# Attention, Fourier mixing and a feed-forward on one core: tying the squares of the scale passes to the feed-forward

## The chip, the core and the metric

One core of a Trainium2 chip. The metric is the device time of one execution in microseconds (us), and a kernel is judged by the median of several executions. The core's engines are named as in the profile: PE is TensorE (PEld its weight loads), DVE is VectorE, ACT is ScalarE, POOL is GpSimd, SP is SyncE, which here only issues DMAs. Each engine works through a queue of its own in order, and a name with a q (ACTq, SPq) is the queue's own work.

## What is computed

For 8 batches with 8 heads, 576 positions and head width 64, cut to what matters:

```python
scores = scale * q @ k.T + bias            # causal, window of 128 positions
x = softmax(scores) @ v                    # heads joined: [8, 576, 512]
u = x + real(fft2(x))                      # over positions and channels
un = (u - mean(u)) / sqrt(var(u) + 1e-6)
out = u + relu(un @ w1) @ w2               # w1 [512, 2048], w2 [2048, 512]
```

## The kernel before, in words

The kernel keeps products exact enough by splitting each operand into two f16 halves, so most products are three matmuls. For that every tensor has to be scaled to a good range first. For batches 2 to 7 a **scale pass** (`batch_scales`, line 254) reads q, k and v of the batch once ahead of time, in 15 pieces of up to 512 columns (5 of q, 5 of k, 5 of v):

- `fetch` (line 266) takes one of the slots in `mslots` (three of them once the second weight is ready, otherwise two), and SP loads a piece into it. For batches 3 to 7 a one-element POOL copy at line 272 first writes into the slot from `last[-1]`, the output of the last emitted attention weighting (line 491, DVE). The load writes the same slot, so it can't start before that copy.
- `part` (line 275) frees the slot in the plan and issues one ACT Square over the piece in place (line 278), with the sum of each row put in one column of the tile `mx`. A sum read-out (ACTIVATION_READ_ACCUMULATOR) goes with it.
- `top` and `scale` (lines 280 and 285) reduce `mx` on DVE (line 282), sum it over partitions with one matmul, and make the batch's scales; the batch's conversions to f16 (line 378) need them.

The **feed-forward** (`ffn`, line 735) goes over row sets of 256 (for odd batches also one of 128). Per row set it first makes blocks of 512 columns in one of two PSUM banks `fp` (line 752, 24 matmuls each). Each block is emptied by an ACT rectification (line 757) into one of eight slots of `hbuf`, and by a DVE subtraction that reads the bank and the rectified half and writes the second half (it runs through the helper at line 169). Only then can PE use the bank again. After the blocks of a row set, the second product (line 767) runs, in which there are no rectifications. Its sums leave the same two banks through a DVE instruction into `X` or `ut`. The bursts of line 752 and of line 767 alternate, each half as long as a row set.

**What sets the order.** All parts of the program are put into one heap with due times (`put`, line 165) and emitted in order of these. The unit of the due times is a planner's step: one pair of heads takes 6 of them and one batch 24. For batch b > 2 the k-th square is due at T + 24(b - 2) - 0.163 + 1.152 k (from `SB`, `SE`, `begin_of`, with T = `T1`), and the load of that piece 1.9 x 1.152 earlier. At that time the feed-forward of batch b - 3 is being emitted; its steps begin at T + 24(b - 2) + 0.432 and come every 24/64 (even batches) or 24/80 (odd ones), and the m-th rectification of its first burst falls on step 2m + 1, counted from m = 0. The order of emission is not the order in the queues: the framework places each engine's instructions at build time from a simulated timeline, in which an instruction goes into its queue when what it needs is there (`schedule_with_timeline_sim=True`, line 932). So a square can stand in ACT's queue ahead of rectifications that were emitted before it.

Around them on ACT are the exponentials of the attention (line 169), the first halves of their f16 pairs (line 428), conversions (line 378) and evictions of the Fourier products (lines 606 and 644 to 648). On SP are the loads and the DMA transposes of attention weights (line 437) and of normalised rows (line 729). POOL has little else: the copies of line 272, memsets (lines 263 and 642) and a power of the normalisation (line 712).

Of the kernel before, what the change touches and what calls it, by code (L numbers as in the profile page):

```python
# [22 lines left out]
NF = 2  # L23
# [59 lines left out]
def attn_fft_ffn_kernel(  # L83
# [16 lines left out]
    V, A, G, T = nc.vector, nc.scalar, nc.gpsimd, nc.tensor  # L100
# [40 lines left out]
    def w1_ap(e, c, f):  # L141
        g, o = divmod(f, 2)
        return wf[0][:, g, e, o * 512 + c * 128:o * 512 + c * 128 + 128]

    def w2_ap(e, f):
        g, o = divmod(f, 2)
        return wf[1][:, g, e, o * 512:(o + 1) * 512]
# [4 lines left out]
    def total(m):  # L152
        sums = ps_d.tile([128, 512], F32, name="pd")[:, 0:m.shape[1]]
        T.matmul(sums, misc[:, 7:8].broadcast_to([128, 128]), m, start=True, stop=True)
        return sums

    def root_inv(dst, src):
        V.tensor_scalar(dst, src, 0.5, 2.0 ** -81, ALU.mult, ALU.max)
        V.tensor_scalar(dst.bitcast(I32), dst.bitcast(I32), 1, 0x3F800000, ALU.logical_shift_right, ALU.bitwise_and)
        V.reciprocal(dst, dst)  # L160
# [4 lines left out]
    def put(t, f, *a):  # L165
        heappush(queue, (t, next(order), f, a))

    def after(dt, f, *a, **kw):
        put(now[0] + dt, lambda: f(*a, **kw))  # L169
# [3 lines left out]

    ready = set()
    weighed, valued = [0] * B, [0] * 4 * B
    last = []

    def weights(wi, t0, dt, t1, dt1):
        w, top = ((w1, 2.0 ** 7), (w2, 2.0 ** 14))[wi]
# [70 lines left out]
    def x_scales(sc, gi, r):  # L250
        V.tensor_scalar_mul(sc[:, 5:6], r, 2.0 ** -53)
        V.reciprocal(gi[:, 1:2], sc[:, 5:6])
        V.tensor_scalar_mul(sc[:, 6:7], gi[:, 1:2], 2.0 ** -3)
        V.tensor_scalar_mul(sc[:, 7:8], gi[:, 1:2], 2.0 ** -11)
# [3 lines left out]
    def batch_scales(b, t0, dt):  # L258
        box = {}

        def begin():
            box["mx"] = small.tile([128, 3, 5], F32, name="mx", tag="mx")
            G.memset(box["mx"], 0.0)

        def fetch(x, fl, o, n):
            assert (0, 7) in ready
            slot = next(turns) % (3 if (1, 7) in ready and b > NF else 2)
            assert slot not in held
            held.add(slot)
            box[x] = slot, mslots[slot][:, 0:n]  # L270
            if b > NF:
                G.tensor_copy(box[x][1][0:1, 0:1], last[-1])  # L272
            nc.sync.dma_start(out=box[x][1], in_=fl[:, o:o + n])

        def part(x, i, c):
            slot, t = box.pop(x)
            held.discard(slot)
            A.activation(t, t, AF.Square, accum_out=box["mx"][:, i, c:c + 1])  # L278

        def top():  # L280
            m1 = small.tile([128, 3], F32, name="m1")
            V.tensor_reduce(m1, box["mx"], AX.X, ALU.max)
            box["sums"] = total(m1)

        def scale():
            r = small.tile([128, 3], F32, name="r")
            root_inv(r, box["sums"])
            sc = small.tile([128, 8], F32, name="sc", bufs=3)
            V.tensor_scalar_mul(sc[:, 0:1], r[:, 0:1], 2.0 ** -58)
            V.tensor_scalar_mul(sc[:, 1:3], r[:, 1:3], 2.0 ** -51)  # L290
            V.scalar_tensor_tensor(sc[:, 3:4], sc[:, 0:1], 8.0, sc[:, 1:2], ALU.mult, ALU.mult)
            gi = small.tile([128, 8], F32, name="gi")
            V.reciprocal(gi[:, 0:1], sc[:, 3:4])
            nsl = small.tile([128, 12], F32, name="nsl")
            V.tensor_scalar(nsl[:, 0:8], slope_sb[:, 0:8], gi[:, 0:1], None, ALU.mult)
            V.tensor_scalar(nsl[:, 8:12], slope_sb[:, 8:12], sc[:, 0:1], None, ALU.mult)
            rg = att.tile([128, 1152], BF16, name="rg", bufs=2)
            A.activation(rg, rel_sb, AF.Copy, scale=sc[:, 3:4])
            x_scales(sc, gi, r[:, 2:3])
            scs[b] = sc, nsl, rg  # L300

        put(t0 - 2.5 * dt, begin)
        x = 0
        for i, (src, n) in enumerate(((q, NQ * 4), (k, NK * 4), (v, 2560))):
            fl = src[b].rearrange(("j p s -> (j p s)", "h p c d -> (h p c d)")[i == 2])
            fl = fl.rearrange("(p x) -> p x", p=128)
            for c, o in enumerate(range(0, n, 512)):
                put(t0 + dt * (x - (FL if b > NF else min(FL, 1.95))), fetch, x, fl, o, min(512, n - o))
                put(t0 + dt * x, part, x, i, c)
                x += 1  # L310
        put(t0 + dt * x, top)
        put(t0 + dt * x + 0.6, scale)
# [424 lines left out]
    def ffn(b):  # L737
        X = Xs[b]
        parts = [(uTs[b][i], 256, [X[:, XS[2 * i]], X[:, XS[2 * i + 1]]], 4 * b + 2 * i) for i in range(2)]
        if b % 2 == 1:  # L740
            parts.append((uTs[b][2], 128, [uts[b // 2]], 4 * B + b // 2))
        for uT, n, tiles, slot in parts:
            per = 512 // n
            hh = []
            assert (b, id(uT)) in ready
            for f0 in range(0, 16, per):
                assert (0, (f0 + per - 1) // 2) in ready
                fp = ps_f.tile([128, 512], F32, name="fp")
                for i in range(per):
                    for c in range(4):  # L750
                        for p, (e, j) in enumerate(((0, 0), (0, 1), (1, 0))):
                            T.matmul(fp[:, i * n:(i + 1) * n], w1_ap(e, c, f0 + i), uT[:, j, c, 0:n],  # L752
                                     start=(c == 0 and p == 0), stop=(c == 3 and p == 2))
                    if i == per // 2 - 1:
                        yield
                ht = next(hslots)
                A.activation(ht[:, 0], fp, AF.Relu)  # L757
                after(0.2, V.scalar_tensor_tensor, ht[:, 1], fp, 0.0, ht[:, 0], ALU.max, ALU.subtract)
                for i in range(per):
                    hh.append(ht[:, :, i * n:(i + 1) * n])  # L760
                yield
            for i, t in enumerate(tiles):
                op = ps_f.tile([128, 512], F32, name="fp")
                for f in range(16):
                    assert (1, f // 2) in ready
                    for p, (a, e) in enumerate(((0, 0), (0, 1), (1, 0))):
                        T.matmul(op, hh[f][:, a, i * 128:(i + 1) * 128], w2_ap(e, f),  # L767
                                 start=(f == 0 and p == 0), stop=(f == 15 and p == 2))
                    if f % 2 == 1 and f < 15:
                        yield  # L770
                after(0.15, V.scalar_tensor_tensor, t, op, wone, t, ALU.mult, ALU.add)
                after(0.4, nc.sync.dma_start, out=ov[slot + i], in_=t)
                yield


    for p in range(4 * B):
        b, j = divmod(p, 4)
# [31 lines left out]
    for b in range(B):  # L809
        t = begin_of(4 * b)  # L810
        if b >= NF:
            batch_scales(b, *((t - SA, SD) if b == NF else (t - SB, SE)))
        fourier(b, transform_of(b))
        n = 80 if b % 2 else 64
        t = forward_of(b)
        put(t, step, ffn(b), t, (24 if b else forward_of(1) - t - E0) / n)
# [118 lines left out]
```

## Time and profile before

| what | value |
|---|---|
| median of 3 runs | 1081.24 us (1079.13 to 1081.65) |
| span of the profiled execution | 1083.9 us |
| PE busy in it | 1039.0 us (96%) |
| DVE, ACT, POOL busy | 703.2, 583.0, 48.0 us |
| squares of line 278 | 90 (75 of them of batches 3 to 7) |
| copies of line 272 | 75 |

The profiled execution's own time is known by its span alone, 1083.9 us from the first to the last instruction, which is 2.7 us (0.25%) above the median of the runs. A row of instructions reads: line, engine, operation, tile written <- tiles read, size, count; a bracket behind it gives how long its engine had been idle before it and what released it. In the table of stretches the columns are busy us and instruction count of each engine, then PEclk, the TensorE clock granted as a share of full speed (1.0 is 2.4 GHz, 0.5 is 1.2 GHz), and the DMA share.

### The profile page before, as it was taken

The page shows a single profiled execution, that of the slowest core. Times are in us where ns is not written, and L with a number is a line of the kernel's source. Part 1 is how long each engine was busy: PE and PEld are TensorE (multiplying, and loading weights), DVE is VectorE, ACT ScalarE, POOL GpSimd, SP SyncE. Part 2 cuts the span into 40 slices and gives each one's busy share as a digit, 9 for nine tenths or more (in the row PEclk, how much of TensorE's full clock was granted, in tenths as well). Part 3 has the DMA queues.
Part 4 walks back from the last instruction along what each step waited for, and adds up shares of the span by engine and source line. Part 5 has one row for each costly group of instructions (what it writes and reads, how often), then busy time and mean ns, then how long its engine had stood idle before and what let it go on. Part 6 is the DMA issues. An engine that isn't in the chain of part 4 may idle for free.

```text
span 1083.9 us, 23935 instructions
## 1 busy us (share of the span) xinstructions
PE 1039.0 (96%) x9208; PEld 726.4 (67%) x9208; DVE 703.2 (65%) x2073; ACT 583.0 (54%) x1388; POOL 48.0 (4%) x136
## 2 busy tenths in 40 slices
PE   8998889899899999999899999999999999999998
PEld 5876776675667667675657667584757676757655
DVE  4889789687674868687674858678784836252111
ACT  6886987558444567567554556556544522241000
POOL 0000001000000000001100000001000000000000
PEclk8998989999999999999999999999999999999999
DMA  9961466727542364527643364537522330030000
GB/s 365 346 218 56 123 147 158 151 54 187 136 101 75 97 147 123 147 51 152 170 109 74 96 146 119 143 54 134 110 60 34 53 69 11 10 60 11 20 10 21
DMA packets 191506, 117.81 MB, mean 109 GB/s; under 512 B 154400, under 2 KB 164128, under 8 KB 191392
## 3 DMA queue, kind: packets, MB, share of 16 engines
q1 hardware_dynamic: 190816, 114.84, 42.4%
q8 instruction: 72, 1.18, 0.5%
q10 hardware_dynamic: 576, 1.45, 0.3%
q14 instruction: 42, 0.34, 0.1%
HBM read 70.63 MB, written 9.44 MB: 74 GB/s over the span
## 4 chain that ended last, share of the span: by engine, by line
PE 61%; DVE 16%; DMA 9%; ACT 7%; issue 3%; SPq 2%; POOL 1%; ACTq 0%; DVEq 0%; POOLq 0%
PE fp L752 25%; PE fp L767 22%; PE sp L403 4%; DMA wall<-v_dram 4%; DVE P L415 2%; DMA wall<-q_dram 2%; ACT wall L278 2%; PE pd L602 2%; PE pv L468 2%; DVE P L169 1%; PE pd L636 1%; DVE hbuf L169 1%; DMA pt<-P 1%; ACT P L169 1%; PE sp L446 1%
## 5 line engine op out<-in xcount | busy, mean ns | idle before, releaser
L767 PE MATMUL fp<-wall,hbuf 128*128 128x512 f16 x1728 | 391.2, 379 | 0.0
L752 PEld LDWEIGHTS <-wall 128*128 128x128 f16 x3840 | 338.5, 99 | 70.4 <-issue 25.2
L752 PE MATMUL fp<-uT,wall 128*128 128x256 f16 x3072 | 365.4, 275 | 20.2 <-DVE hbuf L169 11.9
L767 PEld LDWEIGHTS <-hbuf 128*128 128x128 f16 x1728 | 162.8, 98 | 184.9 <-issue 3.5
L757 ACT ACTIVATE hbuf<-fp 128x512 f16<-128x512 f32 x144 | 84.8, 589 | 202.0 <-PE fp L752 201.9
L169 ACT ACTIVATE P<-P,nb 128x256 f32<-128x256 f32 x320 | 141.9, 477 | 60.8 <-DVE nb L415 60.5
L169 DVE SCALAR_TENSOR_TENSOR hbuf<-fp,hbuf 128x512 f16<-128x512 f32 x144 | 98.8, 686 | 99.3 <-ACT hbuf L757 98.4
L169 DVE SCALAR_TENSOR_TENSOR P<-P 128x256 f16<-128x256 f32 x240 | 87.4, 391 | 40.4 <-ACT P L428 38.9
L415 DVE CUSTOM_DVE_ANT_0 P<-sp,rg,nsl 128x256 f32<-128x256 f32 x240 | 97.5, 449 | 13.7 <-PE sp L403 12.0
L278 ACT ACTIVATE wall<-wall 128x512 f32<-128x512 f32 (+2 forms) x90 | 54.4, 605 | 91.3 <-DMA wall<-k_dram 33.5
L403 PE MATMUL sp<-kk,qq 64*128 64x256 f16 (+5 forms) x880 | 95.0, 287 | 1.4 <-ACT pt L449 0.7
L428 ACT ACTIVATE P<-P 128x256 f16<-128x256 f32 x240 | 84.1, 382 | 2.4 <-DMA pt<-P 1.7
L473 PE MATMUL pv<-vhs,pt 128*128 128x65 f16 x432 | 56.0, 195 | 1.2 <-DMA pt<-P 1.1
L474 PE MATMUL pv<-vl,pt 128*128 128x64 f16 x432 | 55.9, 193 | 0.0
L169 DVE SCALAR_TENSOR_TENSOR X<-fp,misc,X 128x512 f32<-128x512 f32 x32 | 23.8, 744 | 48.4 <-PE fp L767 48.3
L475 PE MATMUL pv<-vhs,pt 128*128 128x65 f16 x432 | 55.1, 194 | 0.0
L403 PEld LDWEIGHTS <-qq 64*128 64x128 f16 (+1 forms) x720 | 32.4, 99 | 24.6 <-issue 18.8
L473 PEld LDWEIGHTS <-pt 128*128 128x128 f16 x432 | 41.0, 98 | 9.6 <-issue 1.3
L752 PE MATMUL fp<-wall,wall 128*128 128x128 f16 x768 | 46.2, 219 | 0.0
L474 PEld LDWEIGHTS <-pt 128*128 128x128 f16 x432 | 40.7, 99 | 6.1
L468 PEld LDWEIGHTS pv<-vr,pt 128*128 128x128 f32 x288 | 37.6, 199 | 6.1 <-PE pv L323 3.3
L272 POOL COPY wall<-X 1x1 f32<-1x1 f32 x75 | 26.2, 377 | 343.9 <-DVE X L491 265.0
(159 smaller groups left out, 1205.9 us busy)
## 6 DMA issues: line engine op xcount, KB each, us to landing
qr<-q_dram SPq DMA_DIRECT2D x32, 304.0 KB, 3.2
hbuf<-w_dram SPq DMA_DIRECT2D x16, 512.0 KB, 7.7
out_dram<-X SPq DMA_DIRECT2D x32, 256.0 KB, 2.2
wall<-v_dram SPq DMA_DIRECT2D x30, 256.0 KB, 3.5
vr<-v_dram SPq DMA_DIRECT2D x24, 320.0 KB, 4.1
kr<-k_dram SPq DMA_DIRECT2D x24, 289.0 KB, 3.8
wall<-q_dram SPq DMA_DIRECT2D x24, 256.0 KB, 3.0
wall<-k_dram SPq DMA_DIRECT2D x24, 256.0 KB, 3.1
```

The source lines that it names most:

```text
L169: put(now[0] + dt, lambda: f(*a, **kw))
L278: A.activation(t, t, AF.Square, accum_out=box["mx"][:, i, c:c + 1])
L403: T.matmul(sp[e][:m, col:col + n], qq[h, c0:c0 + m], keys(kk[h], ti), start=(x == 0), stop=(x == len(prods) - 1))
L415: V.tensor_tensor_reduce(pt[:m, 0:n], sp[e][:m, col:col + n], tab[:m, pc:pc + n], mul, 3.0e38, ALU.add, ALU.min, nb[:m, ti:ti + 1])
L428: A.activation(hi, P32, AF.Copy, scale=2.0 ** 14)
L468: T.matmul(pv[:, ti], pt[:, col:col + 128], ops[p][2][:, e, vc], start=first, stop=last)
L473: T.matmul(pv[:, ti], ph, vh[:, e, vc], start=first, stop=False)
L474: T.matmul(pv[:, ti, 0:D], ph, vl[:, e, vc], start=False, stop=False)
L475: T.matmul(pv[:, ti], pl, vh[:, e, vc], start=False, stop=last)
L752: T.matmul(fp[:, i * n:(i + 1) * n], w1_ap(e, c, f0 + i), uT[:, j, c, 0:n], start=(c == 0 and p == 0), stop=(c == 3 and p == 2))
L757: A.activation(ht[:, 0], fp, AF.Relu)
L767: T.matmul(op, hh[f][:, a, i * 128:(i + 1) * 128], w2_ap(e, f), start=(f == 0 and p == 0), stop=(f == 15 and p == 2))
```

## The change

Every square of batches 3 to 7 gets a one-element POOL copy in front of it. It reads one element of the last rectification that was emitted, and writes it to the element of `mx` into which the square then puts its first row's sum. So the square can't be placed before that rectification and the copy. The list `pace` collects the rectified tiles in order of emission.

```diff
-    last = []
+    last, pace = [], []
...
         def part(x, i, c):
             slot, t = box.pop(x)
             held.discard(slot)
+            if b > NF:
+                G.tensor_copy(box["mx"][0:1, i, c:c + 1], pace[-1])
             A.activation(t, t, AF.Square, accum_out=box["mx"][:, i, c:c + 1])
...
                 ht = next(hslots)
                 A.activation(ht[:, 0], fp, AF.Relu)
+                pace.append(ht[0:1, 0, 0:1])
                 after(0.2, V.scalar_tensor_tensor, ht[:, 1], fp, 0.0, ht[:, 0], ALU.max, ALU.subtract)
```

## Rows read from the trace of the kernel before

**Rows 1.** The page, part 1: busy us, share of the span, instructions of each engine

```profile
PE 1039.0 (96%) x9208; PEld 726.4 (67%) x9208; DVE 703.2 (65%) x2073; ACT 583.0 (54%) x1388; POOL 48.0 (4%) x136
```

**Rows 2.** Waits of PE, 195 to 735 us: us in total, times, longest us

```profile
PE fp L752 <- DVE hbuf L169: 11.9, 10, 2.7
PE fp L752 <- DVE ut L169: 3.5, 2, 2.5
PE pd L602 <- DVE zl L610: 3.5, 3, 2.1
PE fp L752 <- DVE X L169: 2.0, 2, 1.4
PE pv L473 <- DMA pt<-P: 1.1, 1, 1.1
PE pd L602 <- ACT fh L575: 0.8, 1, 0.8
```

**Rows 3.** Line 278, 145 to 735 us: ACT's idle us before it, times

```profile
  DMA wall<-k_dram: 33.5, 17
  DMA wall<-q_dram: 28.4, 13
  DMA wall<-v_dram: 26.3, 12
```

**Rows 4.** Timeline of ACT, 395.5 to 403.9 us: start us, us, instruction

```profile
397.30 0.63 ACT L278 ACTIVATE wall<-wall 128x512 f32<-128x512 f32 x1 [4.32 <-DMA wall<-q_dram]
...
400.31 0.57 ACT L757 ACTIVATE hbuf<-fp 128x512 f16<-128x512 f32 x1
403.20 0.60 ACT L757 ACTIVATE hbuf<-fp 128x512 f16<-128x512 f32 x1 [2.32 <-PE fp L752]
```

**Rows 5.** Timeline of SP's queue, 388 to 398 us

```profile
390.22 2.63 SPq L729 DMA_TRANSPOSE uT<-un  x2
```

**Rows 6.** ACT's idle time before line 278, 391.55 to 424 us, then 449 to 453 us

```profile
  DMA wall<-q_dram: 6.1, 2
  DMA wall<-k_dram: 3.3, 2
...
  DMA wall<-v_dram: 6.0, 2
```

**Rows 7.** Timeline of PE: four places between 275 and 650 us

```profile
275.19 2.79 PE L752 MATMUL fp<-uT,wall 128*128 128x256 f16 x24
...
280.86 2.41 PE L752 MATMUL fp<-uT,wall 128*128 128x256 f16 x12 [2.67 <-DVE hbuf L169]
...
511.82 0.38 PE L752 MATMUL fp<-uT,wall 128*128 128x256 f16 x2 [1.44 <-DVE X L169]
...
646.07 4.45 PE L752 MATMUL fp<-uT,wall 128*128 128x256 f16 x24 [2.48 <-DVE ut L169]
```

**Rows 8.** Busy time by stretch: 645.2 to 648.6 us

```profile
645.20:648.60 3.40, 2.53 (x14) 1.88 (x14) 2.04 (x5) 1.37 (x5) 0.00 (x0) 0.68 0.89 253
```

**Rows 9.** The page, part 5: the copies of line 272 (busy us, mean ns, POOL idle)

```profile
L272 POOL COPY wall<-X 1x1 f32<-1x1 f32 x75 | 26.2, 377 | 343.9 <-DVE X L491 265.0
```

**Rows 10.** The page, part 6: loads of k's pieces (count, KB, us to landing)

```profile
wall<-k_dram SPq DMA_DIRECT2D x24, 256.0 KB, 3.1
```

**Rows 11.** Timeline of POOL, 535 to 540 us

```profile
535.31 3.39 POOL L272 COPY wall<-X 1x1 f32<-1x1 f32 x2 [18.41 <-DVE X L491]
```

**Rows 12.** Timeline of DVE, 535.9 to 538.8 us

```profile
537.04 0.67 DVE L538 TENSOR_TENSOR fg<-X 128x512 f32<-128x512 f32 x1
```

**Rows 13.** Timeline of ACT: the end of batch 5's pass and a later rectification

```profile
452.51 0.19 ACT L278 ACTIVATION_READ_ACCUMULATOR wall<-wall 128x1 f32 x1
...
470.68 0.60 ACT L757 ACTIVATE hbuf<-fp 128x512 f16<-128x512 f32 x1 [0.96 <-PE fp L752]
```

**Rows 14.** Timeline of DVE: the reduction and the scales of batch 5

```profile
452.73 0.17 DVE L282 TENSOR_REDUCE m<-mx 128x3 f32<-128x15 f32 x1 [6.28 <-ACT wall L278]
...
481.03 0.15 DVE L159 TENSOR_SCALAR r<-r 128x3 int32<-128x3 int32 x1
```

## The prediction

> **What bounds the kernel.** The page first: PE is busy for 96% of the span, ACT for 54%, POOL for 4% [rows 1]. So only PE's gaps can be won or made longer. PE's waits come next, in the stretch where batches 3 to 7 are scaled [rows 2]: 22.8 us in all. Most end with the DVE instruction that frees a feed-forward bank (11.9, 3.5 and 2.0 us) or with a Fourier half that waits for ACT (3.5 us).
>
> Then the view of line 278, to see what ACT was doing: before the 75 squares of batches 3 to 7 ACT sat idle for 33.5 + 28.4 + 26.3 = 88.2 us, each time until a load had landed [rows 3]. The timelines join the two. At 397.30 a square of batch 5 starts after 4.32 us of waiting for q's piece. Its load was late because SP had been issuing two transposes for 2.63 us [rows 5]. Behind it in ACT's queue stand work of the attention and the rectification of 400.31 [rows 4]. The same picture stands ahead of 280.86 us, where PE's next block starts 2.67 us late [rows 7].
>
> These gaps have a second price. After the two longest, 2.67 and 2.48 us [rows 7], the granted clock fell: 0.68 over the mean of one 3.4 us stretch, so part of it at 1.2 GHz instead of 2.4 [rows 8]. There 24 matmuls took 4.45 us where they take 2.79 at full clock [rows 7]: 1.7 us more, about 3.3 us for the two places.
>
> **Which squares move.** I worked out from the due times which rectification each square is tied to, and looked where both stand in ACT's queue. Example, batch 5, third q piece (k = 2): due at T + 72 + 2.14. Rectifications of batch 2's first burst are due at T + 72 + 0.81, 1.56, 2.31. So it is tied to the second, which ran at 403.20, while the square ran at 397.30: it moves past two rectifications and 5.9 us [rows 4]. So done for all 75, 50 squares stand ahead of their rectification (6 in batch 3, 11 in each of the others), by one to six rectifications and mostly 5 to 20 us. The other 25 are tied to one that ran long before, since they fall into bursts of line 767, and the tie does nothing. Of the waiting, 59.0 us stand before the 50 (4.8, 12.4, 15.4, 11.2, 15.1 us by batch) and 29.4 us before the 25. Batch 5 shows the reading: 6.1 + 3.3 us before its squares 1 to 8 and 6.0 us before the last three are its 15.4 us [rows 6].
>
> **What that takes away.** Of PE's 22.8 us I leave out three waits: 1.44 us at 511.82, where no square had waited for 5 us before [rows 7], and the 1.1 and 0.8 us for transposed weights and a Fourier input [rows 2]. The remaining 19.5 us follow, in the timelines, on a wait of one of the 50 squares. With the clock that is 19.5 + 3.3 = 22.8 us, the most the change can give back. The exchange rate from ACT to PE is 19.5 / 59.0 = 0.33: two thirds of ACT's waiting is hidden behind PE's second bank. The 29.4 us before the other squares cost PE nothing that I can see, and stay.
>
> **What it adds.** 75 POOL copies. POOL has time (mean 377 ns, 26 us for 75 [rows 9]), so they cost nothing there. Their price is that a moved square now stands in ACT's queue until rectification, copy and hand-overs are done, and the next exponential or rectification stands behind it. No row of before shows ACT waiting for such a copy. The lower bound is nothing, when ACT has other work in between. The upper is a square right behind its rectification: 377 ns and about 0.1 us for two hand-overs (DVE starts 0.03 us after the read-out of the last square ends [rows 13, 14]). I take that upper value, 50 x 0.48 = 24 us of ACT, since ACT is often idle just before it, and 0.33 of it for PE: 8 us. If PE hid none of it, it would be 24 us; if all, 0. Below nothing it can't be, since the order's own gain is already counted.
>
> **What is late next.** A square frees its slot later, and the load three pieces on waits for it. Most such loads wait longer for the weighting anyway: POOL sat idle 265.0 us for line 491 before line 272 [rows 9]. Where two squares three apart hang on neighbouring rectifications (the ninth piece of batches 4 to 7, tied to the end of a burst) the load starts only then. With 3.1 us to landing [rows 10] and SP's issue of up to 2.6 us [rows 5], each may bring back 2 to 4 us of ACT: some 12 us, or 4 us for PE. SP's queue holds the transposes of line 437 behind a load that waits. That risk is in the kernel already, as the load waits for POOL now too, and I cost it at nothing. It would cost PE a wait for transposed weights, of which there are 1.1 us now [rows 2].
>
> **The end of the pass** is covered. In batch 5 the last three squares move from before 452.70 to behind the rectification of 470.68 [rows 13], so the reduction comes near 473 instead of 452.73. The first instruction that needs its result starts at 481.03 [rows 14], held up by the single bank of the Fourier products, so 8 us are left. Batches 4 and 6 have more. The eight slots of `hbuf` now have a third reader, whose copy runs long before the slot comes round: nothing.
>
> **Sum.** 22.8 - 8 - 4 = 10.8 us less. The profiled span would go from 1083.9 to 1073; its offset of 2.7 us to the median stays, so the median goes from 1081.24 to about 1071 us. As the queues are placed anew at build time, other instructions will shift too. I have no row to size that; it is the blur in the bounds. With nothing lost the time is 1058; with 24 us for the copies and 4 for loads it is 1086.
>
> **The rivals.** A measurement of this kernel can tell 0.3% (3.2 us) from no change.
>
> *The waits come back* (no change). The slot chain makes every load as late as its square, or the squares behind a rectification wait for something else, so ACT idles as long. For it: three slots, and loads that already land late through SP [rows 5]. Against: the 5 to 20 us by which squares move are more than their waits of 1 to 5 us. If half of the 22.8 us goes and copies and loads cost 8 + 4 us, the change is about nil: 1081 us.
>
> *The copy holds ACT* (slower). POOL's queue is in order, too. A copy of line 272 waits in it up to 18.41 us for a weighting, and two copies there took 3.39 us [rows 11] while DVE ran a series of instructions with two SBUF inputs [rows 12]. If a rectification's copy stands behind these, the square and everything after it in ACT's queue stand still. The point of decision is a mean hold of 22.8 / (50 x 0.33) = 1.4 us per moved square, against the 0.48 I took. At 2 us it costs 33 us and gives 1081.2 + 10 = 1091 us. Against it: the builder puts POOL's copies in the order in which their inputs arrive in its timeline, and the mean copy was 0.377 us.
>
> A rule speaks for this rival. The Trainium skill (SBUF — State Buffer, "SBUF: two separate sides") says that DVE and GpSimd share a port pair as an exclusive lock, so that a GpSimd operation fully blocks behind a DVE instruction with two SBUF inputs. By that rule a copy takes as long as the DVE run beside it, and rows 11 and 12 agree. By it the sum would be slower only if most copies met such runs, as few of the 75 did, which their mean says.
>
> *The tie does nothing*, so the order stays. The copy's input and output are tracked like any other, so I give this almost nothing; it would be the no-change case.
>
> **How the numbers follow.** My forecast, faster, has 0.64: the waits are seen in rows and the moved squares are far from their loads. No change has 0.15, slower by more than 0.3% has 0.21. The likeliest time is 1071.0 us. The range reaches from 1060 (copies almost free) to 1087, which holds the no-change case and about half of the slower one. The forecast's own range is 1060 to 1078.
>
> **What would show it.** Right: ACT's idle time for loads before line 278 falls from 88 to some 40 us, the squares stand behind rectifications in the timeline, waits for POOL before line 278 stay near 25 us in all, PE's waits for `hbuf`, `X`, `ut` and `zl` fall from 20.9 to some 10 us, and the clock holds at 280 and 646 us. Wrong: long idle times of ACT released by line 278's copy, or as much waiting for loads as now; or PE waits elsewhere, for transposed weights or scales, because the new order is worse in a place that these rows do not show.

## The result, and the profile after

| | before | after |
|---|---|---|
| median (4 runs each, side by side) | 1080.18 us (1075.72 to 1081.65) | 1063.87 us (1061.70 to 1068.52) |
| ratio after / before | | 0.986, 95% interval 0.983 to 0.989 |
| span of the profiled execution | 1083.9 us | 1059.9 us |

The change makes the kernel faster by 16.3 us between the medians; the ratio's interval says 12 to 18 us. The prediction said 1071.0 us, so it had the sign and the mechanism, and its gain was some 6 us too small. The two profiled executions differ by more than the medians do, 24.0 us in their spans: that of after took 1061.70 us, the shortest of its four runs, and the span of before lies 2.7 us above the median it is set beside in the prediction. In the new kernel the square is line 280, the new copy line 279, the rectification line 759, the first product line 754, the second line 770, the transposes of normalised rows line 731 and the attention weighting line 493.

The page, part 1, of after (busy us, share of the span, instructions; against [rows 1]):

```profile
PE 1036.0 (98%) x9208; PEld 724.8 (68%) x9208; DVE 704.2 (66%) x2073; ACT 585.6 (55%) x1388; POOL 76.6 (7%) x211
```

PE has the same work in less time. ACT's idle time before the squares of batches 3 to 7 (us, times), after, against [rows 3]:

```profile
  DMA wall<-k_dram: 15.0, 11
  POOL mx L279: 14.0, 27
  DMA wall<-q_dram: 4.2, 4
  DMA wall<-v_dram: 4.0, 2
```

The waits for loads fell from 88.2 to 23.2 us. Square by square, those before the 50 squares that move fell from 59.0 to 3.1 us; before the other 25 about 20 of 29.4 us are left. New are 14.0 us of waits for the copy. PE's waits from 195 to 735 us (us in total, times, longest), after, against [rows 2]:

```profile
PE pv L475 <- DMA pt<-P: 3.2, 1, 3.2
PE pv L475 <- DVE X L493: 1.9, 1, 1.9
PE fp L754 <- DVE X L169: 1.5, 1, 1.5
PE pd L604 <- DVE zl L612: 0.7, 1, 0.7
PE pd L604 <- ACT fh L577: 0.4, 1, 0.4
```

All ten waits for `hbuf` and both for `ut` are gone, and the sum went from 22.8 to 7.7 us. The timeline of ACT, batch 5's third q piece, in place of [rows 4]:

```profile
393.49 0.60 ACT L759 ACTIVATE hbuf<-fp 128x512 f16<-128x512 f32 x1 [1.03 <-PE fp L754]
394.36 0.63 ACT L280 ACTIVATE wall<-wall 128x512 f32<-128x512 f32 x1 [0.27 <-POOL mx L279]
```

The same square that had stood ahead of its rectification, 4.32 us in wait for its load, now stands right behind it. The load is there, and the square waits 0.27 us for the copy. All 50 now stand behind their rectifications; 27 of them wait for the copy, and one of batch 3 still waits 3.1 us for its load.

Where the time came from, by stretch: busy us (instructions) of PE, PEld, DVE, ACT, POOL, then PEclk, DMA share and GB/s. Before:

```profile
250.00:370.00 120.00, 112.58 (x990) 75.62 (x988) 77.11 (x229) 66.27 (x163) 5.81 (x18) 0.99 0.46 116
370.00:490.00 120.00, 117.27 (x1203) 84.29 (x1201) 90.25 (x270) 74.15 (x189) 6.34 (x21) 1.00 0.48 118
490.00:610.00 120.00, 115.42 (x1018) 76.25 (x1017) 82.92 (x252) 66.40 (x163) 10.22 (x21) 1.00 0.50 118
610.00:730.00 120.00, 116.05 (x1172) 83.41 (x1170) 85.53 (x250) 71.05 (x181) 5.24 (x19) 0.99 0.50 119
```

After:

```profile
250.00:370.00 120.00, 116.72 (x1095) 80.55 (x1094) 82.97 (x239) 69.34 (x169) 9.98 (x32) 0.99 0.52 124
370.00:490.00 120.00, 119.99 (x1159) 82.39 (x1156) 94.48 (x292) 78.93 (x195) 17.01 (x41) 1.00 0.55 123
490.00:610.00 120.00, 118.50 (x1152) 82.85 (x1151) 84.12 (x248) 68.85 (x170) 10.78 (x31) 1.00 0.53 120
610.00:730.00 120.00, 119.98 (x1131) 81.02 (x1129) 93.97 (x284) 79.92 (x194) 16.38 (x37) 1.00 0.53 125
```

PE gains 2.7 to 4.1 us in each; in two of the four it has no gap left. The clock, after, behind the one long gap that remains (3.20 us, ending at 264.02) and from there to the end of the stretch:

```profile
264.00:268.20 4.20, 4.09 (x30) 2.94 (x31) 3.68 (x14) 2.91 (x8) 0.17 (x1) 0.59 0.87 202
268.20:735.00 466.80, 464.78 (x4442) 319.74 (x4440) 346.04 (x1036) 286.05 (x705) 53.12 (x138) 1.00 0.53 120
```

The drops to 1.2 GHz at 281 and 646 us, 3.3 us together, are gone; one at 264 us is new and costs 0.41 x 4.2 = 1.7 us. So the account is 22.8 - 7.7 = 15.1 us of waits and 3.3 - 1.7 = 1.6 us of clock: 16.7 us, against 16.3 measured. That the two are so near is in part luck. The account covers 195 to 735 us of the two profiled executions, and these lie 24.0 us apart: 4.7 us of it are there already at the rectification that starts at 168.49 us before and at 163.83 us after, ahead of the stretch. In the other trace of the changed kernel (told next) PE waits 7.1 us, but the clock is at 1.2 GHz from 211.6 to 215.0 and from 266.3 to 269.7 us, so there no clock is won. The waits are the part that both traces show.

### The profile page after: what moved, and what is told of

It is laid out like the page before. It is cut to its first block, busy times and chain, and to the rows that moved or that the text cites. A ratio compares the mean times of both kernels' runs of the same rounds, so it can differ in the third digit from the quotient of the medians.

```text
span 1059.9 us, 24024 instructions
## 1 busy us (share of the span) xinstructions
PE 1036.0 (98%) x9208; PEld 724.8 (68%) x9208; DVE 704.2 (66%) x2073; ACT 585.6 (55%) x1388; POOL 76.6 (7%) x211
## 4 chain that ended last, share of the span: by engine, by line
PE 67%; DVE 6%; ACT 2%; DMA 1%; issue 1%; POOL 1%; SPq 0%; DVEq 0%; POOLq 0%; ACTq 0%
PE fp L754 30%; PE fp L770 28%; PE sp L405 3%; PE pd L604 2%; PE pv L475 1%; DVE P L417 1%; PE pd L638 1%; PE pv L477 1%; PE pv L476 1%; DMA wall<-q_dram 1%; DVE st L711 1%; DMA uT<-un 1%; PE pd L621 0%; DVE P L169 0%; ACT P L430 0%
## 5 line engine op out<-in xcount | busy, mean ns | idle before, releaser
L280 ACT ACTIVATE wall<-wall 128x512 f32<-128x512 f32 (+2 forms) x90 | 54.5, 605 | 40.2 <-DMA wall<-k_dram 15.3
L477 PE MATMUL pv<-vhs,pt 128*128 128x65 f16 x432 | 54.5, 194 | 0.0
L272 POOL COPY wall<-X 1x1 f32<-1x1 f32 x75 | 30.1, 420 | 221.3 <-DVE X L493 152.0
L470 PE MATMUL pv<-vr,pt 128*128 128x65 f32 x288 | 43.0, 291 | 0.4 <-ACT pt L451 0.3
```

What stands on the lines that cost most here:

```text
L470: T.matmul(pv[:, ti], pt[:, col:col + 128], ops[p][2][:, e, vc], start=first, stop=last)
L477: T.matmul(pv[:, ti], pl, vh[:, e, vc], start=False, stop=last)
```

## The experiments

Each is the changed kernel with one edit; lines of an edit that only prepare it are left out (...). Ratios are to the kernel before, run on the same chip beside it (its medians: 1081.15 us beside the first four kernels told here; 1080.53 us beside batches 3 to 5, 0.9 of a pitch, squares without loads and the mix; 1078.94 us beside the other three).

**The change once more**, without an edit, to have it beside the others.

> The changed kernel itself, run beside the variants so that they can be compared on one chip. All theories: about 1064 us, ratio near 0.986.

Measured: 1063.78 us, ratio 0.982 (0.979 to 0.986); ACT waits 14.4 us for copies and 23.2 for loads, PE 7.1 us.

**The order without the copy.** The square is held behind the same rectification by an order of issue alone, so it needs nothing from POOL.

```diff
-            if b > NF:
-                G.tensor_copy(box["mx"][0:1, i, c:c + 1], pace[-1])
-            A.activation(t, t, AF.Square, accum_out=box["mx"][:, i, c:c + 1])
+            with tc.issue_after(pace[-1]) if b > NF else ExitStack():
+                A.activation(t, t, AF.Square, accum_out=box["mx"][:, i, c:c + 1])
...
-                pace.append(ht[0:1, 0, 0:1])
+                pace.append(relu.ins)
```

> No POOL copies; each square of batches 3 to 7 is only queued on ACT behind the rectification to which the copy tied it (an edge of order, no wait). Theory order (the gain comes from the squares' place behind the rectifications, where their loads have landed): gains at least as much as the change. By my exchange rate of 0.33 the 14 us that ACT waits for copies are worth 4.6 us, so about 1059 us; if PE hides these waits wholly, about 1064. Rival copy (the pacing through POOL is what helps): back at about 1080.

Measured: 1071.67 us, ratio 0.990 (0.987 to 0.994). That is a miss: the order was as meant, the waits for loads were 24.7 us and those for copies none, and yet it lost half of the gain. From 310 us on its stretches are as full as the change's; the loss is in batch 4's first 60 us. The stretch from 250 to 310 us, this kernel:

```profile
250.00:310.00 60.00, 50.64 (x431) 34.52 (x430) 48.76 (x154) 41.70 (x96) 7.74 (x13) 0.94 0.69 154
```

and the change:

```profile
250.00:310.00 60.00, 56.72 (x482) 37.30 (x481) 43.47 (x123) 35.45 (x83) 7.12 (x20) 0.97 0.66 150
```

6.1 of the 7.9 us are here. PE's three longest gaps in this stretch, this kernel:

```profile
265.34 4.45 PE L754 MATMUL fp<-uT,wall 128*128 128x256 f16 x24 [3.41 <-DVE hbuf L169]
...
281.94 0.21 PE L475 MATMUL pv<-vhs,pt 128*128 128x65 f16 x1 [1.59 <-DMA pt<-P]
...
293.98 6.35 PE L770 MATMUL fp<-wall,hbuf 128*128 128x512 f16 x22 [3.50 <-DVE hbuf L169]
```

and the only long one of the change:

```profile
264.02 0.20 PE L475 MATMUL pv<-vhs,pt 128*128 128x65 f16 x1 [3.20 <-DMA pt<-P]
```

The first gap is not the loss, since the change has one of that length there. Ahead of it ACT waited for a q load of the attention in both kernels:

```profile
261.90 0.80 ACT L380 ACTIVATE qq<-qr,nsl 128x608 f16<-128x608 f32 x1 [3.47 <-DMA qr<-q_dram]
```

in this kernel, and in the change:

```profile
259.80 0.80 ACT L380 ACTIVATE qq<-qr,nsl 128x608 f16<-128x608 f32 x1 [3.88 <-DMA qr<-q_dram]
```

The loss is the other two, with the clock behind the last (this kernel, 290 to 300 us; the change has 10.00 us of PE and 1.00 there):

```profile
290.00:300.00 10.00, 6.50 (x28) 2.78 (x27) 9.94 (x26) 7.34 (x20) 2.70 (x4) 0.83 0.62 161
```

1.59 + 3.50 us and 0.17 x 10 = 1.7 us of clock are 6.8 of the 7.9 us. Ahead of the last gap the rectification ended at 291.09, but DVE began the subtraction only at 293.24, behind conversions and Fourier folds in its queue. No square stands in that path. What made the transposed weights late is not followed here. So the order holds the squares as well as the copy does; the loss comes from a new placement of other work. Why the builder chose it stays open.

**The copies without the order.** The copy reads the weighting that the fetch had waited for anyway, so the squares stand where they stood before, 50 ahead of their rectification.

```diff
-            box[x] = slot, mslots[slot][:, 0:n]
+            box[x] = slot, mslots[slot][:, 0:n], last[-1] if last else None
...
-                G.tensor_copy(box["mx"][0:1, i, c:c + 1], pace[-1])
+                G.tensor_copy(box["mx"][0:1, i, c:c + 1], tied)
```

> All 75 copies, but each reads the element that the square's own load was already tied to, so it is ready long before and the squares stand where they stood (50 ahead of their rectification, as before). Theory order: no gain, 1080 us within 4; ACT's waiting for loads near 88 us. Rival luck (any new placement of the queues gives such a gain): 1062 to 1072 us.

Measured: 1078.15 us, ratio 0.997 (0.9949 to 0.9996). ACT's idle time before the squares:

```profile
  DMA wall<-v_dram: 25.8, 12
  DMA wall<-q_dram: 25.6, 12
  DMA wall<-k_dram: 24.9, 13
  POOL mx L279: 9.5, 3
```

The load waits are back (76.3 us), and PE's with them (18.6 us, 9.7 of these for `hbuf`). A copy alone, or merely building the program anew, gives 0.3%, not 1.4%.

**Four copies in a row.** Three more one-element copies behind each, in place on `mx`: a longer hold and nothing else.

```diff
-                G.tensor_copy(box["mx"][0:1, i, c:c + 1], pace[-1])
+                G.tensor_copy(box["mx"][0:1, i, c:c + 1], pace[-1]); [G.tensor_copy(box["mx"][0:1, i, c:c + 1], box["mx"][0:1, i, c:c + 1]) for _ in range(3)]
```

> Each copy of the change followed by three more one-element POOL copies onto the same element, so the square is held longer: at 0.17 to 0.4 us each some 0.5 to 1.2 us more for those right behind their rectification, about 14 to 25 us more waiting of ACT on 27 to 50 squares. By the exchange rate of 0.33 that costs 5 to 8 us: 1069 to 1072 us. Rival (such short waits right behind a rectification are hidden by PE's second bank): 1064 us within 3.

Measured: 1073.20 us, ratio 0.992 (0.988 to 0.995); ACT's idle time for the copies:

```profile
  POOL mx L279: 49.3, 34
```

35 us more of hold than the change's 14.4, not the 14 to 25 expected, cost 9.4 us, or 0.27 of it. That is not yet the prediction's 0.33, which sets PE's waits against ACT's: PE's waits grew by 5.3 us (13.0 against 7.7), a rate of 0.15, and none of them ends with `hbuf`. Which wait makes up the rest is not shown.

**The tie in batches 3 to 5 alone.**

```diff
-            if b > NF:
+            if NF < b < 6:
```

> The copies in batches 3 to 5 alone; the squares of 6 and 7 stand as in the kernel before (22 of the 50 ahead of their rectification). Theory order: the gain is made batch by batch. Before, PE's waits behind squares of batches 6 and 7 were some 6 to 8 of the 19.5 us, with one of the two clock drops, so 28 of 50 ties give 55 to 65% of the gain: 1070 to 1072 us, and the second half of the trace waits as before. Rival luck (one good placement somewhere): either about 1064 or about 1081 us.

Measured: 1073.54 us, ratio 0.994 (0.991 to 0.996). Two of its stretches:

```profile
370.00:490.00 120.00, 119.98 (x1186) 83.65 (x1184) 94.87 (x288) 76.79 (x190) 15.12 (x39) 1.00 0.52 120
490.00:610.00 120.00, 114.96 (x1032) 77.37 (x1029) 77.94 (x232) 67.66 (x168) 8.80 (x18) 0.99 0.49 118
```

Where the batch's squares are tied PE is full as in the change (119.99); in the first stretch where they are not it is as before (115.42), in the last one in between (117.57 us; 116.05 before, 119.98 in the change). So the gain goes with the batches that are tied. Its size was missed: 7.0 us are some 43% of the change's 16.3, where 55 to 65% were expected.

**Loads due later: 0.9 of a square's pitch ahead instead of 1.9.**

```diff
-                put(t0 + dt * (x - (FL if b > NF else min(FL, 1.95))), fetch, x, fl, o, min(512, n - o))
+                put(t0 + dt * (x - (0.9 if b > NF else min(FL, 1.95))), fetch, x, fl, o, min(512, n - o))
```

> The change with one constant moved: for batches 3 to 7 a piece's load is due 0.9 instead of 1.9 squares ahead. The squares still stand behind their rectifications, but with about half the time for the load. Theory order (what counts is that the load has landed when the square's turn comes): ACT waits for loads again, some 40 to 90 us before line 280, and at 0.2 to 0.33 of it the time goes to 1072 to 1085 us. Rival place (standing behind a rectification is what helps, whatever the square then waits for): 1064 us within 3 although ACT waits.

Measured: 1065.82 us, ratio 0.986 (0.983 to 0.989), within the change's interval. It missed its purpose: of 37.2 us of load waits only 8.7 stand before squares that move. The other loads still landed before the rectification that their squares now follow. So it was pushed further:

**Loads due 0.2 of a pitch ahead.**

```diff
-                put(t0 + dt * (x - (FL if b > NF else min(FL, 1.95))), fetch, x, fl, o, min(512, n - o))
+                put(t0 + dt * (x - (0.2 if b > NF else min(FL, 1.95))), fetch, x, fl, o, min(512, n - o))
```

> The change with each load of batches 3 to 7 due 0.2 of a square's pitch ahead of its square (about 1.2 us) instead of 1.9. The 0.9 of the earlier run was still early enough for the squares that move. Theory (the gain comes from loads that have landed): the squares stand behind their rectifications as in the change, but find loads that are still on their way; ACT's waits for loads before the squares come to 60 us or more (23 us in the change), PE's waits from 195 to 735 us to 14 us or more (7.7 us), and the time to 1072 us or more. Rival (it is the place behind a rectification that counts, not the landed load): 1064 us, give or take 3, whatever ACT waits for loads.

Measured: 1074.93 us, ratio 0.995 (0.993 to 0.998). No square stands ahead of its rectification, and still most of the gain is lost. ACT's idle time before the squares:

```profile
  DMA wall<-q_dram: 27.3, 11
  DMA wall<-v_dram: 20.2, 8
  DMA wall<-k_dram: 15.0, 10
  POOL mx L279: 12.7, 16
```

26.4 of these 62.5 us for loads stand before the 50 squares. One of them in the timeline:

```profile
516.24 0.63 ACT L280 ACTIVATE wall<-wall 128x512 f32<-128x512 f32 x1 [5.43 <-DMA wall<-q_dram]
...
519.38 0.57 ACT L759 ACTIVATE hbuf<-fp 128x512 f16<-128x512 f32 x1
...
520.74 4.40 PE L754 MATMUL fp<-uT,wall 128*128 128x256 f16 x24 [3.66 <-DVE hbuf L169]
```

It is the picture of before again: a square in wait for its load, the next rectification behind it, PE's bank late, and the clock down over the next 24 matmuls. PE's waits are 16.6 us, 8.9 more than the change's; 26.4 - 3.1 = 23.3 us of ACT at 0.33 would be 7.7.

**Squares without loads.** They read a resident table and write to a scrap tile, so they never wait for a load, and an order of issue places them up to three rectifications early. The loads still run, but nothing reads them, so a load no longer waits for the square that last used its slot, and the scales are not those of the batch. The copies of the change are left out.

```diff
-            if b > NF:
-                G.tensor_copy(box["mx"][0:1, i, c:c + 1], pace[-1])
-            A.activation(t, t, AF.Square, accum_out=box["mx"][:, i, c:c + 1])
+            there, src = (junk[:, 0:t.shape[1]], tab2_sb[:, 0, 0:t.shape[1]]) if b > NF else (t, t)
+            with tc.issue_after(pace[-4]) if b > NF else ExitStack():
+                A.activation(there, src, AF.Square, accum_out=box["mx"][:, i, c:c + 1])
...
```

> The kernel before, with the squares of batches 3 to 7 reading a table that lies in the memory (and writing to a scratch tile) instead of the loaded piece, which is left unread; on ACT each is queued behind the fourth last rectification, so most stand three rectifications ahead of where the change puts them, as early as before, but with nothing to wait for. Theory order: no waiting for loads, so most of the gain: 1062 to 1068 us. Rival place (a square ahead of a rectification delays it by its own 0.72 us, and this is what costs): 1075 us or more.

Measured: 1064.97 us, ratio 0.985 (0.982 to 0.989), though 69 of 75 squares stand ahead of their rectification and ACT waits for nothing before any of them. So without the wait the place costs nothing that can be measured; the change is already as good as squares that never wait.

**Copies in batches 3 and 4, the order of issue in 5 to 7**, to have the change's placement in the disputed stretch and no copies later.

```diff
-            if b > NF:
-                G.tensor_copy(box["mx"][0:1, i, c:c + 1], pace[-1])
-            A.activation(t, t, AF.Square, accum_out=box["mx"][:, i, c:c + 1])
+            if NF < b < 5:
+                G.tensor_copy(box["mx"][0:1, i, c:c + 1], pace[-1][0])
+            with tc.issue_after(pace[-1][1]) if b >= 5 else ExitStack():
+                A.activation(t, t, AF.Square, accum_out=box["mx"][:, i, c:c + 1])
...
```

> The copies in batches 3 and 4, the edge of order without copy in batches 5 to 7. The run with edges alone lost some 8 us against the change, and its trace shows them all between 250 and 310 us (batch 4). Theory order: the copies themselves do nothing, so here 1064 us within 3, and ACT's waits for POOL fall to some 2 us. Rival copy (the delay that the copy adds helps in every batch): 1068 us or more.

Measured: 1067.21 us, ratio 0.987 (0.983 to 0.990). The copies' waits fell to 1.9 us, and nothing was gained by that. But ACT's waits for loads rose from 23.2 to 30.2 us, so this does not show by itself that 12 of the change's 14 us cost PE nothing. And with the copies back in batches 3 and 4, the loss of the kernel without copies is gone from the stretch of 250 to 310 us (PE busy 56.47 us).

**Copies for the 50 squares alone.**

```diff
-            if b > NF:
+            if b > NF and 5 * i + c in ((0, 1, 3, 12, 13, 14), (*range(1, 7), *range(10, 15)), (*range(1, 9), 12, 13, 14))[0 if b == 3 else 1 + b % 2]:
```

> The change with the copies in front of the 50 squares alone that had stood ahead of their rectification; the 25 others have none. Theory (the tie does nothing for the 25): 1064 us, give or take 3, and ACT's waits for copies near 14 us as in the change. Rival (the 25 copies hold some of their squares too, or keep an order that would otherwise fall apart): 1067 us or more, with squares ahead of their rectification again.

Measured: 1065.01 us, ratio 0.986 (0.983 to 0.989); 11.4 us of waits for copies, one square, one of the 25, ahead of its rectification. The 25 others' copies do nothing for the time.

**Tied to the last rectification but one.**

```diff
-                G.tensor_copy(box["mx"][0:1, i, c:c + 1], pace[-1])
+                G.tensor_copy(box["mx"][0:1, i, c:c + 1], pace[-2])
```

> The change with each copy reading the last rectification but one. Every square may come one rectification (some 3 us) earlier, and its copy has run before. Theory (the load decides, and most squares had moved by more than one rectification): 1062 to 1069 us, ACT's waits for copies under 5 us, for loads 25 to 45 us. Rival (the place directly behind the last rectification is what counts): 1071 us or more. A third reading, that the copies' hold of 14 us costs PE a rate of 0.27, makes it up to 3.8 us faster than the change where the loads still land in time: 1060 us.

Measured: 1064.47 us, ratio 0.986 (0.982 to 0.989). 49 squares stand one rectification ahead of the place that the change gives them; load waits are 38.5 us, some 6 of them before the 50, and copies 8.4 where under 5 were expected. The 1060 us of the third reading did not come. A step back of one rectification, some 3 us, leaves the loads landed and the gain whole. No version beat the change.

All of it in one table: ACT's idle time before the 75 squares (loads and copies), PE's waits from 195 to 735 us, the ratio.

| kernel | ACT, us | PE, us | ratio |
|---|---|---|---|
| squares without loads | 0 | 9.2 | 0.985 |
| order without the copy | 24.7 | 13.7 | 0.990 |
| mix | 32.1 | 8.6 | 0.987 |
| the change (again) | 37.2 (37.6) | 7.7 (7.1) | 0.986 (0.982) |
| copies for the 50 | 38.8 | 10.7 | 0.986 |
| last but one | 46.9 | 7.2 | 0.986 |
| loads 0.9 ahead | 54.5 | 9.5 | 0.986 |
| batches 3 to 5 | 62.4 | 15.5 | 0.994 |
| four copies | 72.0 | 13.0 | 0.992 |
| loads 0.2 ahead | 75.2 | 16.6 | 0.995 |
| copies without the order | 85.8 | 18.6 | 0.997 |
| before | 88.2 | 22.8 | 1 |

## Why the prediction was right, and where its sum was off

**What bounds the kernel, and which squares move:** held. PE's gaps came from loads that were late for squares. Taking the waits away without the order (squares without loads) gives the whole gain, and bringing them back under the new order (loads 0.2 ahead) takes most of it. The count of 50 held too: copies for these alone do it all. The signs that were named came, and went further than said: ACT's waits for loads are 23.2 us, not some 40, those for copies 14.0, not 25, and PE's for `hbuf`, `X` of the feed-forward, `ut` and `zl` 2.2, not 10.

**What that takes away:** 19.5 us of waits and 3.3 us of clock. Of the 19.5 us 0.7 are left, and both clock drops went. But the waits that were left out did not stay at 3.3 us: they came to 7.0, since for transposed weights there are now 3.2 us (at 264 us) instead of 1.1 (at 669 us) and one wait for line 493 (1.9 us) is new; and behind the first the clock fell (1.7 us). Given back are 0.7 + 3.7 + 1.7 = 6.1 us, in places that no row of before sized. The gap at 264 us belongs to the new order: the other trace of the change has 2.83 us there, and the variants whose squares move have 2.5 to 4.4 us, under one releaser or another; the kernel before has 2.03 us there, behind a square.

**The exchange rate** of 0.33 held for waits of its own kind: 8.9 / 23.3 = 0.38 for the later loads. For the longer hold of the copies PE's waits give 0.15. It doesn't hold for every wait, either. Leaving out the order without the copy, whose loss has another cause, the table has six kernels from 0 to 55 us of ACT's waiting with 7 to 11 us of PE's; those above 60 us have 13 to 23. What ACT still waits in the change is hidden from PE.

**The terms that were mis-sized** are the two that were charged. The copies: 24 us of ACT and 8 us of PE were taken, 0.48 for each of 50; measured are 14.0 us. The size was right for a square that waits (14.0 / 27 = 0.52), but 23 of the 50 did not wait at all, which the prediction had as its lower bound. A square right behind its rectification mostly waits 0.27 us: the 0.1 us for hand-overs held, but a copy takes 0.17 us and not the 0.377 us that is the mean of line 272 with its few long ones. At rates of 0.15 to 0.38 the 14.0 us would be 2 to 5 us of PE; no run sizes it more closely, and the mix without most of them was no faster. The renewed load waits: 12 us of ACT and 4 of PE were taken, at the ninth pieces of batches 4 to 7; those wait 1.6, 0, 2.1 and 0 us, and the 50 squares 3.1 us in all. With 6 us given back in place of 8 + 4, the sum of 10.8 becomes the 16.7 us of the account above.

**The rivals.** The waits did not come back. The copy did hold ACT in places, as that rival said. The timeline of batch 5, after:

```profile
410.42 1.90 POOL L279 CAST mx<-hbuf 1x1 f32<-1x1 f16 x1 [2.25 <-ACT hbuf L759]
...
410.65 0.67 DVE L540 TENSOR_TENSOR fg<-X 128x512 f32<-128x512 f32 x1
...
412.35 0.63 ACT L280 ACTIVATE wall<-wall 128x512 f32<-128x512 f32 x1 [2.00 <-POOL mx L279]
```

A copy that takes 0.17 us elsewhere took 1.90 us beside a run of DVE's instructions with two SBUF inputs, and ACT stood 2.00 us. But all copies of line 279 (min/median/max ns, first and last start in us):

```profile
L279 POOL CAST mx<-hbuf x75: 173/174/2192, 164.5 to 695.9; 1x1 f32<-1x1 f16 x75
```

The median is the bare 0.17 us, and 7 of the 75 took over 1 us; the mean hold of 14.0 / 50 = 0.28 us is far from the 1.4 us at which that rival wins. The trace agrees with the lock that the Trainium skill (SBUF — State Buffer, "SBUF: two separate sides") describes, and says how seldom it was met here.

**The end of the pass** is covered, with less to spare than said. The timelines of DVE and PE, after, against [rows 14]:

```profile
461.03 0.16 DVE L284 TENSOR_REDUCE m<-mx 128x3 f32<-128x15 f32 x1
466.60 0.36 PE L154 MATMUL pd<-m,misc 128*128 128x3 f32 x2
468.82 0.15 DVE L159 TENSOR_SCALAR r<-r 128x3 int32<-128x3 int32 x1
```

The reduction starts 7.8 us ahead of line 159, where 8 were foretold. But line 159 is not the first to need its result: the matmul of line 154 that sums it over partitions is, at 466.60 (478.81 before), so 5.4 us are left after the reduction's end.

## What to carry to other kernels

An in-order engine that serves the bottleneck must not hold an instruction whose load may be late ahead of one that frees a bank. Such an instruction can be tied behind work that is known to come later than the load, at the price of one small instruction, if its result is not due soon; what counts is that the load has landed, not the exact place. Ask of each wait whether a bank behind it runs dry: here the last 37 us of ACT's waits were worth nothing that could be measured.

## What the runs showed beside that

A new placement moves work far from the edit: the same order of squares, made without the copy, cost 7.9 us more, mostly through two gaps of PE, one behind transposed weights and one behind a DVE subtraction that stood late in its queue. Only PE's gaps of both kernels side by side tell these from the first long gap, which the change has too. And long gaps of PE cost more than their length: behind those of 3.20, 3.41 and 3.66 us shown here the clock stood at 1.2 GHz for a while (0.59 over 4.2 us; 24 matmuls in 4.45 and 4.40 us where they take 2.79).
